# A Fourier mixing layer and hash-routed experts: another order of the head

## The chip, the cores and the metric

The kernel runs on one core of a Trainium2 chip. The metric is the device time of one execution in microseconds; the median of three runs is compared. The core has five engines that run their own instruction streams in order: TensorE (PE, with its weight loads as PEld), VectorE (DVE), ScalarE (ACT), GpSimd (POOL) and SyncE (SP). SP, ACT and POOL each also issue transfers into a queue of their own.

## The reference

```python
# x (8, 2496, 256); filt_r, filt_i (1249, 256)
X = np.fft.rfft(x, axis=1)
F = (filt_r + 1j * filt_i)[None, :, :]
y = np.fft.irfft(X * F, n=2496, axis=1).astype(np.float32)

x = y.reshape(19968, 256)                 # tokens
expert_idx = token_ids * np.int64(2654435761) % np.int64(8)
for e in range(8):                        # w1 (8, 256, 1024), w2 (8, 1024, 256)
    xe = x[expert_idx == e]
    out[expert_idx == e] = np.maximum(xe @ w1[e], 0.0) @ w2[e]
```

## The kernel before

**The mixing.** The transform of 2496 = 39 × 64 points is cut into three stages of matrix products, for each of 8 batches. *Stage 1* (`stage1`, product `pa`, line 185) multiplies by the 39-point table `wf_t`: eight units per batch, each of two products on one x piece of 312 KB, which ACT copies out (line 187) and stores into a DRAM buffer d1 (line 188, 320 KB). *Stage 2* (`stage2`) runs eleven steps: `forward` (product `pb`, line 202) multiplies groups loaded back from d1 (`load2`, line 194, two transfers of 256 KB per group of four frequencies) by `d_t`, VectorE multiplies by both filters (line 207), and `back` (product `pc`, line 221) multiplies by `e_t`; ACT copies (line 224) and stores into d2 (line 228). *Stage 3* (`stage3`, product `pd`, line 249) has eight units per batch: a piece of d2 (`load4`, line 239, 320 KB) is multiplied by `wi_t`, VectorE copies it out (line 251), and GpSimd scatters its four groups of 78 rows of 1088 bytes into `xs`, rows sorted by expert (`scatter`, line 257). A stage of a batch can start only when the stage before it has stored all of that batch, since its rows lie across. Rings of buffers: x 3, t1 2, t2 4, p 4, g 2, t4 3, o 2, PSUM for all three stages 4.

**The routing.** `route` computes on VectorE, from the token ids, where each token goes: expert ids, a mask that compares with `iota_e` (made on GpSimd, line 315), running counts, and two matmuls on PE for the counts over all partitions (lines 349 and 351, result `cnt_ps`, the second with the matrix `before` from GpSimd). A long chain on VectorE makes the slots of the tokens and stores them for the scatters (lines 397 and 398, GpSimd's queue); at its end `seg` goes through another matmul (line 436, `ce_ps`) into the experts of the 163 tiles, `chunk_i`. `dup_filters` then copies each filter table to the lower partitions, one on VectorE (line 447), one on ACT (line 448).

**The expert tiles.** 163 tiles of 128 tokens run in four stages; the tiles of the first stage (30) hold only tokens of batches 0 and 1, those of the second of batches up to 3, and so on. A tile loads its rows (`load`, line 515, four tiles ahead), turns them on PE (`turn`, line 523, `xps`), multiplies by w1 (`up`, line 534), ReLU on ACT and VectorE, by w2 (`down`, line 546), and scatters the result (line 550). `weights(i + 2, 0)` and `(i + 2, 1)` stand behind `up(i)` and `down(i)` on SP's queue and load 1 MB each if the expert changes; their buffers come free when `up(i)` and `down(i)` have run.

**The order.** It is written out by hand: each engine runs its instructions as the program emits them. `part1`, `part2` and `part3` give the units of a batch's stage a time, and their loads an earlier one; `pre` is the sorted list that is emitted ahead of the tiles, and `main` the one of which the pieces with a time below i + 1 stand in tile i, between `turn(i + 1)` and `down(i)`. `pre` holds batch 0's stage 1, `route`, batch 1's stage 1 mixed with batch 0's stage 2, then batch 1's stage 2 with batch 0's stage 3, then batch 1's stage 3 with batch 2's stage 1. Ahead of `pre`, SP loads `wf_t` and three x pieces, and ACT the token ids, a routing table, `d_t` (1.3 MB), four filter pieces (0.65 MB each), `e_t` (2.6 MB) and `wi_t`.

Of the kernel before, what the change touches and what calls it, by code (L numbers as in the profile page):

```python
# [20 lines left out]
B, S, C = 8, 2496, 256  # L21
# [11 lines left out]
NU = N2 // 2 // XG  # L33
# [75 lines left out]
def kernel(  # L109
# [159 lines left out]
    def weights(i, which):  # L269

        if i >= NT:
            return
        if i < 2:
            if which == 0:
                ws[i] = [wpool.tile([P, DP, F], F32, name=f"w1_{i}"), wpool.tile([P, FP, C], F32, name=f"w2_{i}")]
        elif which == 0:
            ws[i] = ws[i - 2]
        e = nc.sync.value_load(chunk_i[0:1, 0, i:i + 1], min_val=0, max_val=E - 1)
        kw = {}
        if i >= 2:  # L280
            kw = {"cond": nc.sync.value_load(chunk_i[0:1, 1, i:i + 1], min_val=0, max_val=1)}
        if which == 0:
            nc.sync.dma_start(out=ws[i][0][:], in_=moe_w1[bass.ds(e, 1)].rearrange("one (dp p) f -> p (one dp) f", p=P), **kw)
        else:
            nc.sync.dma_start(out=ws[i][1][:], in_=moe_w2[bass.ds(e, 1)].rearrange("one (fp p) d -> p (one fp) d", p=P), **kw)
# [13 lines left out]
    for k, filt in enumerate((filt_r, filt_i)):  # L299
        for q in range(2):  # L300
            off, step = (0, C) if q == 0 else (N1 * C, -C)
            nc.scalar.dma_start(
                out=f_t[k][32 * q:32 * q + 32, :, :],
                in_=bass.AP(tensor=filt.tensor, offset=filt.offset + off,
                            ap=[[N1 * C, 32], [step, NS], [1, C]]))
    nc.scalar.dma_start(out=e_t[:], in_=e_dram.ap())
    nc.scalar.dma_start(out=wi_t[:], in_=wi_dram.ap())

    make_identity(nc, ident[:])
    before = rpool.tile([P, P], F32)  # L310
# [12 lines left out]

        return ap.unsqueeze(2).to_broadcast([P, E, n])

    def route():

        eid_i = rpool.tile([P, NJ], I32)
        nc.vector.tensor_scalar(eid_i[:], tok[:, :, 0], E - 1, None, op0=OP.bitwise_and)
# [2 lines left out]
        mask = rpool.tile([P, E, NJ], F32)  # L332
# [3 lines left out]
        run = rpool.tile([P, E, NJ], F32)  # L336
# [3 lines left out]
        ends = rpool.tile([P, E + 1], F32)  # L340
# [7 lines left out]
        ps = fps.tile([P, 2, C], F32, name="cnt_ps", tag="f")  # L348
        nc.tensor.matmul(out=ps[:, 0, 0:G * E], lhsT=ones[:, 0:P], rhs=cntg[:].rearrange("p g e -> p (g e)"),
                         start=True, stop=True)  # L350
        nc.tensor.matmul(out=ps[:, 1, 0:E], lhsT=before[:], rhs=cnt[:], start=True, stop=True)

        upto = rpool.tile([P, G, E], F32)
# [20 lines left out]
        step = rpool.tile([P, G, E], F32)  # L376
# [33 lines left out]
        at = rpool.tile([P, NQP], F32)  # L410
# [17 lines left out]
        seg = rpool.tile([P, 2], F32)  # L428
# [2 lines left out]
        nc.vector.tensor_copy(seg_i[:], seg[:])  # L431
        nc.vector.tensor_scalar(seg_i[:], seg_i[:], E - 1, None, op0=OP.bitwise_and)
        nc.vector.tensor_copy(seg[:], seg_i[:])
        ps = fps.tile([P, 2, C], F32, name="ce_ps", tag="f")
        for q in range(2):
            nc.tensor.matmul(out=ps[0:1, 0, q * P:(q + 1) * P], lhsT=seg[:, q:q + 1], rhs=ident[:],
# [15 lines left out]
    def part1(b, t0, t1):  # L452
        bt = batches[b]
        at = [t0 + (t1 - t0) * u / NU for u in range(NU)]
        step = (t1 - t0) / NU
        out_ = [(at[u], lambda u=u: bt.stage1(u)) for u in range(NU)]
        out_ += [(at[u] - 1.9 * step, lambda u=u: bt.load1(u)) for u in range(3 if b == 0 else 0, NU)]
        return out_

    def part2(b, t0, t1, ready):  # L460
        bt = batches[b]
        n = NS // 2 + 1
        at = [t0 + (t1 - t0) * u / n for u in range(n)]
        step = (t1 - t0) / n
        out_ = [(at[u], lambda u=u: bt.stage2(u)) for u in range(n)]
        out_ += [(max(at[2 * g] - 4.5 * step, ready), lambda g=g: bt.load2(g)) for g in range(NS // SG)]
        return out_

    def part3(b, t0, t1):
        bt = batches[b]  # L470
        at = [t0 + (t1 - t0) * u / NU for u in range(NU)]
        step = (t1 - t0) / NU
        out_ = [(at[u], lambda u=u: bt.stage3(u)) for u in range(NU)]
        out_ += [(at[u] - 1.9 * step, lambda u=u: bt.load4(u)) for u in range(NU)]
        return out_

    order = stage_tiles()
    tiles = sum(order, [])
    stage_of = [g for g, o in enumerate(order) for _ in o]

    pre = part1(0, -100, -81) + [(-80.9, route), (-80.8, dup_filters)]
    pre += part1(1, -79, -60) + part2(0, -75, -50, -80)
    pre += part2(1, -45, -25, -59) + part3(0, -44, -25)
    pre += part3(1, -20, -1) + part1(2, -19, -2)
    pre += [(-30 + i, lambda i=i: (weights(i, 0), weights(i, 1))) for i in range(2)]
    pre.sort(key=lambda t: t[0])

    bounds = [0.0, 9.0, 18.0, 25.0, 44.0, 63.0, 84.0, 101.0]
    main, ready = [], 0.0
    for k, b in enumerate(range(3, B + 2)):  # L490
        t0, t1 = bounds[k], bounds[k + 1]
        d = t1 - t0
        if b - 1 < B:
            main += part2(b - 1, t0 + 0.01 * d, t0 + 0.9 * d, ready)
        if b < B:
            main += part1(b, t0 + 0.02 * d, t0 + 0.62 * d)
            ready = t0 + 0.65 * d
        if b - 2 >= 2:
            main += part3(b - 2, t0 + 0.3 * d, t1)
    main.sort(key=lambda t: t[0])  # L500

    for _, piece in pre:
# [98 lines left out]
```

## Time and profile before

| | us |
|---|---|
| median of three runs | 1775.54 (1774.68 to 1778.44) |
| the profiled execution | 1772.01 |
| its span, first to last instruction | 1770.3 |
| PE busy | 1665.8 (94%) |
| VectorE, ScalarE, GpSimd busy | 463.8, 222.9, 427.2 |

The span lies 1.7 us below the profiled execution's own time, and that execution 3.5 us below the median. Where a profile row says busy, a fraction of a stretch is meant in which at least one instruction of the engine runs; matmuls overlap at their ends, so the time from start to start is what one adds.

### The profile page before, as it was taken

The page shows a single profiled execution, that of the slowest core. Times are in us where ns is not written, and L with a number is a line of the kernel's source. Part 1 is how long each engine was busy: PE and PEld are TensorE (multiplying, and loading weights), DVE is VectorE, ACT ScalarE, POOL GpSimd, SP SyncE. Part 2 cuts the span into 40 slices and gives each one's busy share as a digit, 9 for nine tenths or more (in the row PEclk, how much of TensorE's full clock was granted, in tenths as well). Part 3 has the DMA queues.
Part 4 walks back from the last instruction along what each step waited for, and adds up shares of the span by engine and source line. Part 5 has one row for each costly group of instructions (what it writes and reads, how often), then busy time and mean ns, then how long its engine had stood idle before and what let it go on. Part 6 is the DMA issues. An engine that isn't in the chain of part 4 may idle for free.

```text
span 1770.3 us, 27290 instructions
## 1 busy us (share of the span) xinstructions
PE 1665.8 (94%) x9630; PEld 1390.9 (79%) x9630; DVE 463.8 (26%) x848; ACT 222.9 (13%) x373; POOL 427.2 (24%) x503
## 2 busy tenths in 40 slices
PE   3398778999999999999999999999999999999998
PEld 0165226887787888888888988898889999999997
DVE  1634212222323322222232222322222111121111
ACT  0231111212111111101110000100000000000000
POOL 0024540012424412230233123233431111111111
PEclk9998659999999999999999999999999999999999
DMA  9378846557667685446463564434516132322220
GB/s 218 101 205 210 261 125 152 160 162 225 184 195 217 175 264 182 128 121 194 123 196 98 160 197 125 123 108 125 187 52 228 62 111 68 104 78 89 83 81 12
DMA packets 159122, 260.72 MB, mean 147 GB/s; under 512 B 18351, under 2 KB 121536, under 8 KB 158667
## 3 DMA queue, kind: packets, MB, share of 16 engines
q1 hardware_dynamic: 108459, 166.93, 32.6%
q10 hardware_dynamic: 29984, 48.70, 9.9%
q0 software_dynamic: 20544, 43.36, 7.5%
q8 instruction: 77, 1.26, 0.3%
q14 instruction: 58, 0.48, 0.1%
HBM read 433.78 MB, written 86.09 MB: 294 GB/s over the span
## 4 chain that ended last, share of the span: by engine, by line
PE 70%; issue 20%; DMA 5%; POOL 3%; DVE 2%; POOLq 0%; ACT 0%; SPq 0%; ACTq 0%; DVEq 0%
PE ups L534 22%; PE dps L546 21%; PE pc L221 8%; PE pa L185 7%; PE pd L249 7%; PE pb L202 4%; POOL out_dram L550 3%; DMA d<-t 2%; PE xps L523 1%; DMA x<-in_x_dram 1%; DMA t<-d 1%; DMA d<-g 1%; DMA w<-in_moe_w_dram 0%; DVE acc L391 0%; DVE tmp L390 0%
## 5 line engine op out<-in xcount | busy, mean ns | idle before, releaser
L534 PEld LDWEIGHTS ups<-xt,w 128*128 128x128 f32 x5216 | 610.2, 192 | 9.3 <-DVE xt L525 0.9
L534 PE MATMUL ups<-xt,w 128*128 128x128 f32 x5216 | 611.0, 276 | 0.5 <-DVE xt L525 0.5
L546 PE MATMUL dps<-w,ht 128*128 128x256 f32 x2608 | 589.8, 379 | 0.0
L546 PEld LDWEIGHTS dps<-w,ht 128*128 128x128 f32 x2608 | 488.5, 190 | 80.3 <-issue 19.2
L550 POOL DMA_INDIRECT out_dram<-osb,xg x163 | 159.9, 981 | 904.7 <-DVE osb L549 878.2
L257 POOL DMA_INDIRECT xs<-o,sidx x256 | 240.9, 941 | 344.4 <-issue 197.6
L540 DVE TENSOR_SCALAR ht<-ups 128x512 f32<-128x512 f32 x163 | 112.8, 692 | 525.8 <-PE ups L534 522.2
L538 ACT ACTIVATE ht<-ups 128x512 f32<-128x512 f32 x163 | 97.3, 597 | 1021.7 <-PE ups L534 998.4
L549 DVE COPY osb<-dps 128x256 f32<-128x256 f32 x163 | 69.3, 425 | 506.7 <-PE dps L546 506.7
L185 PE MATMUL pa<-x,wf_t 78*80 78x512 f32 x256 | 152.2, 731 | 30.5 <-ACT t L187 22.7
L249 PE MATMUL pd<-t,wi_t 80*78 80x512 f32 x256 | 136.2, 658 | 18.8 <-DMA t<-d 18.8
L221 PE MATMUL pc<-p,e_t 128*128 128x256 f32 x640 | 152.2, 381 | 0.2 <-ACT g L224 0.2
L221 PEld LDWEIGHTS pc<-p,e_t 128*128 128x128 f32 x640 | 121.8, 191 | 18.1 <-ACT g L224 0.6
L185 PEld LDWEIGHTS pa<-x,wf_t 78*80 78x80 f32 x256 | 45.1, 181 | 105.2 <-issue 65.8
L207 DVE TENSOR_TENSOR p<-pb,filt 128x512 f32<-128x512 f32 x160 | 103.0, 686 | 87.1 <-PE pb L202 87.0
L251 DVE COPY o<-pd 78x512 f32<-78x512 f32 x128 | 87.6, 686 | 114.0 <-PE pd L249 69.6
L187 ACT COPY t<-pa 80x512 f32<-80x512 f32 x128 | 73.2, 581 | 224.4 <-PE pa L185 199.0
L249 PEld LDWEIGHTS pd<-t,wi_t 80*78 80x78 f32 x256 | 40.1, 163 | 74.1 <-issue 68.5
L202 PEld LDWEIGHTS pb<-t,d_t 128*128 128x128 f32 x320 | 60.8, 195 | 42.9 <-issue 30.8
L202 PE MATMUL pb<-t,d_t 128*128 128x256 f32 x320 | 85.0, 389 | 8.4 <-DMA t<-d 8.4
L224 ACT COPY g<-pc 128x512 f32<-128x512 f32 x80 | 46.8, 585 | 268.4 <-PE pc L221 235.7
L523 PE MATMUL xps<-ident,xg 128*128 128x128 f32 x326 | 62.5, 274 | 8.4 <-DMA xg<-xs 8.4
(76 smaller groups left out, 183.4 us busy)
## 6 DMA issues: line engine op xcount, KB each, us to landing
w<-in_moe_w_dram SPq DMA_DIRECT2D x326, 1024.0 KB
xg<-xs SPq DMA_DIRECT2D x163, 136.0 KB
d<-t ACTq DMA_DIRECT2D x64, 320.0 KB
t<-d SPq DMA_DIRECT2D x80, 256.0 KB
d<-g ACTq DMA_DIRECT2D x80, 256.0 KB
t<-d SPq DMA_DIRECT2D x64, 320.0 KB
x<-in_x_dram SPq DMA_DIRECT2D x64, 312.0 KB
xs<-o,sidx POOLq DMA_INDIRECT x256, 3.2
```

The costliest lines, as they stand in the source:

```text
L185: nc.tensor.matmul(out=ps[0:NK], lhsT=wf_t[:], rhs=xt[:, 2 * i:2 * i + 2, :], start=True, stop=True)
L202: nc.tensor.matmul(out=ps[:, i, :], lhsT=d_t[:, s, :], rhs=self.t2[s // SG][:, s % SG, :], start=True, stop=True)
L207: nc.vector.tensor_tensor(out=pt[:], in0=ps[:], in1=f_t[k][:, 2 * u:2 * u + 2, :], op=OP.mult)
L221: nc.tensor.matmul(out=ps[:, i, :], lhsT=e_t[:, k, 2 * u + i, :], rhs=pr[k][:, i, :], start=(k == 0), stop=(k == 1))
L249: nc.tensor.matmul(out=ps[0:NR], lhsT=wi_t[:], rhs=t4[:, 2 * i:2 * i + 2, :], start=True, stop=True)
L251: nc.vector.tensor_copy(out=o[:, 2 * i:2 * i + 2, 0:C], in_=ps[0:NR])
L257: st = nc.gpsimd.indirect_dma_start(out=xs[:], out_offset=bass.IndirectOffsetOnAxis(ap=index, axis=0), in_=rows, in_offset=None, bounds_ch ...
L534: nc.tensor.matmul(out=ps[:, k, :], lhsT=w1[:, dp, fp * P:(fp + 1) * P], rhs=xt[i][:, dp, :], start=(dp == 0), stop=(dp == DP - 1))
L538: nc.scalar.activation(out=dst, in_=ps[:], func=AF.Relu)
L540: nc.vector.tensor_scalar_max(dst, ps[:], 0.0)
L546: nc.tensor.matmul(out=ps[:], lhsT=ht[:, fp, :], rhs=w2[:, fp, :], start=(fp == 0), stop=(fp == FP - 1))
L550: st = nc.gpsimd.indirect_dma_start(out=out[:], out_offset=bass.IndirectOffsetOnAxis(ap=xg[i][:, C:C + 1].bitcast(I32), axis=0), in_=o[:], ...
```

## The change

The six transfers of the filters, `e_t` and `wi_t` are issued by GpSimd and no longer by ACT. `route` is cut in three: `count` (to the two count matmuls), `route` (the slots, to `seg`) and `experts` (from the `ce_ps` matmul on). `count` and `route` stand behind the first unit of batch 0's stage 1, `experts` late in batch 0's stage 2. In `pre`, stage 1 of batch 2, stage 2 of batch 1 and stage 3 of batch 0 are mixed, and stage 2 of batch 2 with stage 3 of batch 1. Batch 2's stage 3 is now the first of `main`, with batch 3's stage 1, and the times of the other stages among the tiles are written out anew.

```diff
@@ the loads ahead of pre
         for q in range(2):
             off, step = (0, C) if q == 0 else (N1 * C, -C)
-            nc.scalar.dma_start(
+            nc.gpsimd.dma_start(
                 out=f_t[k][32 * q:32 * q + 32, :, :],
...
-    nc.scalar.dma_start(out=e_t[:], in_=e_dram.ap())
-    nc.scalar.dma_start(out=wi_t[:], in_=wi_dram.ap())
+    nc.gpsimd.dma_start(out=e_t[:], in_=e_dram.ap())
+    nc.gpsimd.dma_start(out=wi_t[:], in_=wi_dram.ap())
...
-    def route():
+    rv = {}
+
+    def count():
...
+        rv.update(mask=mask, run=run, ends=ends, ps=ps)
+
+    def route():
+        mask, run, ends, ps = rv["mask"], rv["run"], rv["ends"], rv["ps"]
...
+        rv.update(seg=seg)
+
+    def experts():
+        seg = rv["seg"]
         ps = fps.tile([P, 2, C], F32, name="ce_ps", tag="f")
...
-    def part3(b, t0, t1):
+    def part3(b, t0, t1, ready):
...
-        out_ += [(at[u] - 1.9 * step, lambda u=u: bt.load4(u)) for u in range(NU)]
+        out_ += [(max(at[u] - 1.9 * step, ready), lambda u=u: bt.load4(u)) for u in range(NU)]
...
-    pre = part1(0, -100, -81) + [(-80.9, route), (-80.8, dup_filters)]
-    pre += part1(1, -79, -60) + part2(0, -75, -50, -80)
-    pre += part2(1, -45, -25, -59) + part3(0, -44, -25)
-    pre += part3(1, -20, -1) + part1(2, -19, -2)
+    pre = part1(0, -100, -81) + [(-99, count), (-98.9, route), (-60, experts), (-80.8, dup_filters)]
+    pre += part1(1, -79, -62) + part2(0, -77, -52, -80)
+    pre += part1(2, -50, -30) + part2(1, -50, -25, -61) + part3(0, -48, -27, -51.9)
+    pre += part2(2, -22, -1, -25) + part3(1, -20, -2, -24.9)
...
-    bounds = [0.0, 9.0, 18.0, 25.0, 44.0, 63.0, 84.0, 101.0]
...
+    main = part1(3, 0.1, 6) + part3(2, 0.2, 6, -0.9)
+    main += part2(3, 6.2, 13.5, 6.1) + part1(4, 6.5, 13)
+    main += part2(4, 14.2, 24, 13.2) + part1(5, 14.5, 22) + part3(3, 15, 25, 13.6)
...
```

On GpSimd, at the program's start; rows with a plus are those of the change, line numbers are its own:

```order
+L600 UNCONDITIONAL_BRANCH
+L302 DMA filt_105<-in_filt_r_dram 32x5120
+L302 DMA filt_105<-in_filt_r_dram 32x20x256
+L302 DMA filt_106<-in_filt_i_dram 32x5120
+L302 DMA filt_106<-in_filt_i_dram 32x20x256
+L306 DMA e_t<-e_tbl 128x5120
+L307 DMA wi_t<-wi_tbl 80x78
 masks.py:197 MEMSET ident 128x128
 masks.py:199 ISA
```

Six transfers stand ahead of the identity, and so ahead of `before` and `iota_e`, which follow it.

On PE, from the last unit of batch 0's stage 1 on, in the kernel before (pa and x are followed by the piece's number within its batch):

```order
L185 MATMUL pa_7_0_215<-x_7_202,wf_t 80x512
L185 MATMUL pa_7_1_218<-x_7_202,wf_t 80x512
L349 MATMUL cnt_ps<-cntg,ones 128x32
L351 MATMUL cnt_ps<-cnt,before 128x8
L436 MATMUL ce_ps<-ident,seg 1x128 x2
L185 MATMUL pa_0_0_364<-x_0_212,wf_t 80x512
L185 MATMUL pa_0_1_367<-x_0_212,wf_t 80x512
```

And in the change, from the program's start:

```order
L185 MATMUL pa_0_0_147<-x_0_114,wf_t 80x512
L185 MATMUL pa_0_1_150<-x_0_114,wf_t 80x512
L351 MATMUL cnt_ps<-cntg,ones 128x32
L353 MATMUL cnt_ps<-cnt,before 128x8
L185 MATMUL pa_1_0_275<-x_1_116,wf_t 80x512
L185 MATMUL pa_1_1_278<-x_1_116,wf_t 80x512
```

The count moved from behind the eighth unit to behind the first, and the `ce_ps` matmul, which waited right behind it, into batch 0's stage 2.

On PE, behind the last product of batch 1's stage 2 in the kernel before (the first number of pd, pa, t4 and x is the batch, the second the piece):

```order
L249 MATMUL pd_1_0_0_985<-t4_1_0_975,wi_t_102 78x512
L249 MATMUL pd_1_0_1_988<-t4_1_0_975,wi_t_102 78x512
L185 MATMUL pa_2_0_0_1007<-x_2_0_977,wf_t_101 80x512
L185 MATMUL pa_2_0_1_1010<-x_2_0_977,wf_t_101 80x512
L249 MATMUL pd_1_1_0_1018<-t4_1_1_979,wi_t_102 78x512
L249 MATMUL pd_1_1_1_1021<-t4_1_1_979,wi_t_102 78x512
```

And where batch 2's stage 1 stands in the change, behind batch 0's stage 2:

```order
L185 MATMUL pa_2_1_0_667<-x_2_1_602,wf_t_101 80x512
L185 MATMUL pa_2_1_1_670<-x_2_1_602,wf_t_101 80x512
L202 MATMUL pb_1_2_679<-t2_1_1_589,d_t_103 128x256 x2
L221 MATMUL pc_1_1_686<-p_1_1_0_654,e_t_104 128x256
L221 MATMUL pc_1_1_686<-p_1_1_1_656,e_t_104 128x256
L221 MATMUL pc_1_1_686<-p_1_1_0_654,e_t_104 128x256
L221 MATMUL pc_1_1_686<-p_1_1_1_656,e_t_104 128x256
L249 MATMUL pd_0_1_0_696<-t4_0_1_609,wi_t_102 78x512
L249 MATMUL pd_0_1_1_699<-t4_0_1_609,wi_t_102 78x512
```

Before, units of stages 3 and 1 alternate alone; now each stands among those of stage 2.

## Rows read from the trace of the kernel before

**Rows 1.** The page: PE's busy time, its 40 slices, the granted clock.
```profile
PE 1665.8 (94%) x9630; PEld 1390.9 (79%) x9630; DVE 463.8 (26%) x848; ACT 222.9 (13%) x373; POOL 427.2 (24%) x503
...
PE   3398778999999999999999999999999999999998
...
PEclk9998659999999999999999999999999999999999
```

**Rows 2.** Stretches: length, busy time by engine, granted clock, DMA share, GB/s.
```profile
0.00:57.90 57.90, 27.41 (x32) 7.58 (x33) 5.41 (x9) 9.56 (x16) 1.53 (x11) 1.00 0.86 207
57.90:90.20 32.30, 2.62 (x10) 1.43 (x9) 27.88 (x56) 5.04 (x2) 2.72 (x3) 1.00 0.27 67
90.20:136.10 45.90, 45.63 (x157) 29.72 (x156) 16.86 (x26) 14.76 (x26) 8.71 (x7) 1.00 0.77 216
...
143.55:186.30 42.75, 42.73 (x148) 28.28 (x148) 20.76 (x32) 5.26 (x9) 26.41 (x33) 0.92 0.90 254
186.30:197.55 11.25, 0.00 (x0) 0.03 (x1) 1.28 (x2) 0.58 (x1) 5.33 (x8) 0.74 0.84 264
197.55:252.45 54.90, 54.87 (x64) 16.25 (x64) 10.30 (x15) 9.30 (x16) 27.93 (x36) 0.50 0.62 173
252.45:260.86 8.41, 0.00 (x0) 0.03 (x1) 0.69 (x1) 0.00 (x0) 3.62 (x4) 0.50 0.26 77
260.86:289.00 28.14, 19.21 (x77) 14.61 (x78) 4.03 (x7) 3.51 (x6) 0.00 (x0) 0.77 0.60 139
289.00:1762.30 1473.30, 1473.30 (x9147) 1292.93 (x9145) 374.87 (x697) 174.92 (x297) 349.98 (x402) 1.00 0.47 141
```

**Rows 3.** The timeline of PE among the tiles: start, length, instruction.
```profile
304.34 1.88 PE L185 MATMUL pa<-x,wf_t 78*80 78x512 f32 x4
306.06 1.03 PE L202 MATMUL pb<-t,d_t 128*128 128x256 f32 x4
306.92 1.89 PE L221 MATMUL pc<-p,e_t 128*128 128x256 f32 x8
308.65 1.88 PE L185 MATMUL pa<-x,wf_t 78*80 78x512 f32 x4
...
413.51 1.88 PE L249 MATMUL pd<-t,wi_t 80*78 80x512 f32 x4
```

**Rows 4.** The timeline of ACT in batch 0's stage 1 (brackets: idle before, releaser).
```profile
19.63 0.32 ACTq L307 DMA_DIRECT2D wi_t<-wi_tbl  x1
...
21.28 1.06 ACT L187 COPY t<-pa 80x512 f32<-80x512 f32 x2
...
44.34 1.06 ACT L187 COPY t<-pa 80x512 f32<-80x512 f32 x2 [20.55 <-DMA d<-t]
```

**Rows 5.** The timeline of POOL, VectorE and PE at the routing and the scatters.
```profile
86.25 0.90 POOL L398 DMA_DIRECT2D sidx<-slots  x1 [2.29 <-DMA slots<-slot_i]
...
89.26 1.01 PE L436 MATMUL ce_ps<-ident,seg 128*1 128x128 f32 x4 [29.68 <-DVE seg L433]
...
91.51 2.82 DVE L447 COPY filt<-filt 64x5120 f32<-64x5120 f32 x1
91.57 3.60 POOL L257 DMA_INDIRECT xs<-blank,at_i  x1 [0.30 <-issue]
...
192.20 0.94 POOL L257 DMA_INDIRECT xs<-o,sidx  x1 [0.30 <-issue]
```

**Rows 6.** The timeline of PE and of SP's queue where stages meet.
```profile
97.11 1.91 PE L202 MATMUL pb<-t,d_t 128*128 128x256 f32 x4
...
131.59 3.62 PE L221 MATMUL pc<-p,e_t 128*128 128x256 f32 x16
...
139.94 0.80 SPq L239 DMA_DIRECT2D t<-d  x2
...
143.55 3.67 PE L249 MATMUL pd<-t,wi_t 80*78 80x512 f32 x4 [7.49 <-DMA t<-d]
...
276.75 2.05 PE L202 MATMUL pb<-t,d_t 128*128 128x256 f32 x4 [8.41 <-DMA t<-d]
```

More of the change, by code (lines that the diff above doesn't have):

```diff
@@ L479 @@
     stage_of = [g for g, o in enumerate(order) for _ in o]
-    pre = part1(0, -100, -81) + [(-80.9, route), (-80.8, dup_filters)]
-    pre += part1(1, -79, -60) + part2(0, -75, -50, -80)
-    pre += part2(1, -45, -25, -59) + part3(0, -44, -25)
-    pre += part3(1, -20, -1) + part1(2, -19, -2)
+    pre = part1(0, -100, -81) + [(-99, count), (-98.9, route), (-60, experts), (-80.8, dup_filters)]
+    pre += part1(1, -79, -62) + part2(0, -77, -52, -80)
+    pre += part1(2, -50, -30) + part2(1, -50, -25, -61) + part3(0, -48, -27, -51.9)
+    pre += part2(2, -22, -1, -25) + part3(1, -20, -2, -24.9)
     pre += [(-30 + i, lambda i=i: (weights(i, 0), weights(i, 1))) for i in range(2)]
     pre.sort(key=lambda t: t[0])
-    bounds = [0.0, 9.0, 18.0, 25.0, 44.0, 63.0, 84.0, 101.0]
[L489 to L499, printed above, removed]
+    main = part1(3, 0.1, 6) + part3(2, 0.2, 6, -0.9)
+    main += part2(3, 6.2, 13.5, 6.1) + part1(4, 6.5, 13)
+    main += part2(4, 14.2, 24, 13.2) + part1(5, 14.5, 22) + part3(3, 15, 25, 13.6)
+    for b, t0 in ((5, 25.2), (6, 44.2)):
+        main += part2(b, t0, t0 + 17, t0 - 2) + part1(b + 1, t0 + 0.4, t0 + 12) + part3(b - 1, t0 + 5, t0 + 18.5, t0)
+    main += part2(7, 63.2, 80, 61) + part3(6, 67, 83, 62) + part3(7, 84, 101, 81)
     main.sort(key=lambda t: t[0])
```

## The prediction

> **What bounds the kernel now.** I read the page first: TensorE (PE) is busy 94% of the span and its slices are full from the eighth on; only the first seven are not, and the granted clock is below 1.0 in some of these [rows 1]. So I cut the span at the head's own turning points and took the busy time of each stretch [rows 2]. From 289 us to the last matmul PE is busy 1473.30 of 1473.30 us at clock 1.00. Nothing that the change does there can help; all that can be won is what PE loses before 289.
>
> To price that loss I need the work at the 2.4 GHz level. Among the tiles, from start to start, a stage-1 unit (pa) takes 306.06 − 304.34 = 1.72 us, pb 0.86, pc 308.65 − 306.92 = 1.73 [rows 3]; a stage-3 unit (pd) is as busy as a pa (1.88), so 1.72 too. A batch therefore holds 8 × 1.72 = 13.8 us of stage 1, 10 × 2.59 = 25.9 of stage 2, 13.8 of stage 3: 53.5 in all. Stretch less work gives the **ledger of before** [rows 2]: batch 0's stage 1, 57.9 − 13.8 = 44.1; waiting for the routing, 32.3; stage 1 of batch 1 with stage 2 of batch 0, 45.9 − 40.6 = 5.3; idle 7.5 [rows 6]; stage 2 of batch 1 with stage 3 of batch 0, 42.75 − 38.8 = 3.9; idle 11.25; stage 3 of batch 1 with stage 1 of batch 2, 54.9 − 27.6 = 27.3; idle 8.4; tile 0, with a stretch of 8.41 in which PE waits for stage 2's load [rows 6], 28.1 − 14.3 = 13.8. Sum: **153.8 us lost**. The change is priced by a second ledger with the same units.
>
> **The change, part by part.**
>
> *Stage 1 of batch 0 (A).* In before, ACT hands out six table transfers until 19.95 and copies only from 21.28; its first two stores stand behind the tables in its own queue, and the next copy waits 20.55 us for them [rows 4]. After the change these six stand on POOL, ACT keeps three, and its stores stand behind d_t alone. POOL pays: a plain transfer cost it 0.90 us [rows 5], so six with 0.3 us between them some 7 us, ahead of the identity, `before` and iota_e. The routing's mask needs iota_e, so the count's matmul, now second on PE, comes at about 1 + 7 + 1 + 5.4 (VectorE's nine instructions of the first stretch [rows 2]) = 15; pa_1 to pa_7, queued behind it, start there and no longer right behind pa_0. What binds next is bytes: tokens 0.16 MB, d_t 1.31, filters 2.62, e_t 2.62, x 2.56, stores 2.62, two x units of batch 1 0.64: 12.5 MB. Before moved 207 GB/s in this stretch [rows 2]: 60.5 us with e_t ahead of the stores, 47.9 if e_t comes last. I take 54, plus 4 for the load of stage 2's first group (139.94 to 143.55 in before [rows 6]): pb_0 of batch 0 at **58**. Bounds: 46, where PE's half-speed pace decides (15 + 7 × 3.44 + 3.6 for the load and as much for the last store), and 66. Work done by then is 13.8 + 1.7, so **42.5 lost** (30 to 50).
>
> *The routing.* PE waited 29.68 us for VectorE's chain to end in `seg` [rows 5]. Now this chain runs from about 16 to 46, beside A's transfers; nothing waits for it but the filters' copy and the first products, due at 59. Its cost is 0 while A lasts to 49; the full 29.7 if the count came late (a rival below). So the 32.3 us fall out.
>
> One GpSimd scatter took 3.60 us and not 0.94 beside VectorE's 2.82 us copy of the filters [rows 5]. The Trainium skill (SBUF — State Buffer, section "SBUF: two separate sides") says that such a copy locks GpSimd out of writing descriptors, and advises the ACT or SP queue instead, which speaks against this change; by it as by the row the loss would be 2.7 us on POOL wherever the two meet, and in the first 8 us VectorE has only the two short steps on the token ids to run, so the sum would not move.
>
> *Batch 1's stage 1 with batch 0's stage 2 (B).* The same mixture took 97.11 to 135.2 in before [rows 6] and holds one more unit now. I add 3 for a start at 1.2 GHz: 43 us for 38 of work, **5 lost** (2 to 8). It ends at 101.
>
> *To batch 0's stage 3.* From the last pc's end to the first pd, through store and load, took 143.55 − 135.2 = 8.3 us [rows 6]. Now pa and pb (2.6) fill part: 5.7 idle, and 3 at the lower clock, which the same place shows: **8.7** (6 to 10).
>
> *Three stages mixed (C).* 53.5 us of PE work, 15.8 MB for a batch's three stages, and of the weights' 4.2 MB about half. That is 17.9 MB in some 62 us, 288 GB/s, where the best stretches moved 254 at a share of 0.90 and 264 at 0.84 [rows 2], that is 282 to 314 at a full share. So C is near the limit of the transfers: **6 lost**, between 0 and 22 (all the weights at 254 GB/s).
>
> *To batch 2's stage 2.* SP's queue holds the weights, then batch 2's first groups, then batch 1's load for stage 3. Before paid 11.25 here with the weights just as late; one load group more stands ahead and 3.4 us of work fills: 9 idle and 3 of low clock, **12** (6 to 18).
>
> *Stage 2 of batch 2 with stage 3 of batch 1 (D).* Before lost 3.9 with the same mixture, clock included: **2** (0 to 6). The stretch of stages 1 and 3 alone is gone: there PE was busy 54.87 of 54.9 us at clock 0.50 [rows 2] and lost 27.3.
>
> *To tile 0.* Before needed 8.4 from the end of PE's work; with scatters trailing as at 192.20, 6 us behind the mixture's end [rows 5, 6], it would be 10.5. One pc now stands behind the last pd: **9** (6 to 12).
>
> *Among the tiles.* Batch 2's stage 3 and batch 3's stage 1 now meet in tile 0. SP issues their first loads only once up(0) has freed the weights' buffer. I count 3.4 for up(0) at the lower clock as before, 4.5 for x, and since pa and pd, alternating alone, ran at 1.2 GHz throughout [rows 2], 6.9 for these four and 2.5 for the start of the down product. In tile 6 batch 3's stage 2 is loaded in the tile that uses it, as batch 2's was in tile 0, where 8.41 us were lost [rows 6]: 8 with the clock. Together **25.3** (12 to 32), where before has 13.8.
>
> **Sum:** 42.5 + 5 + 8.7 + 6 + 12 + 2 + 9 + 25.3 = 110.5 against 153.8, a gain of 43.3 us. The profiled execution took 1772.0 (span 1770.3): 1728.7. The median lies 3.5 above that execution, so the forecast is **1732** (1712 to 1752 by the middle of the bounds).
>
> **Rivals.**
>
> *The transfers bind.* The stores of A end with the last table byte wherever tables are issued, C pays for all weights, and the load behind it too: A +8, C +16, the gap +6, 30 us of the 43 given back: **1762**. For it speaks the share of 0.86 in A and 0.90 later [rows 2]; against it, that the copy's 20.55 us were order within one queue, not bytes. The Trainium skill (DMA: Bandwidth & Descriptors, section "Issuing engines are not separate DMA queues") says that all issuers share the same 16 engines and that another issuer saves only issue time; by that rule A would end at the 66 above, and the trace so far shows both, ACT held until 19.95 and bytes at a share of 0.86.
>
> *The gaps fill.* A by its low end (30), no loss in C, 7 behind it, 14 among the tiles: 12.5 + 6 + 5 + 11.3 = 35 more, **1697**. For it: ample work of a third batch at every wait.
>
> *Slower: the lower clock through the mixture.* Where pa and pd stood alone the clock stayed at 1.2 GHz though PE was never idle. In C they are 27.6 of 53.5 us, in B and D a third. If short waits for transfers and this share keep 1.2 GHz through C and D, their remaining 90.6 us double; less the 6 already counted, 85 more: **1817**. It turns the gain into a loss from the point where over half of that work (43 us) runs at 1.2 GHz. Against it, the mixture from 143.55 shows 0.92 over 42.75 us [rows 2]: 6.8 us at 0.50, the rest at 1.00.
>
> *Nothing won: POOL is held as ACT was.* ACT needed until 19.95 for these transfers [rows 4]. If POOL must wait for room until the tables have landed, near 55, iota_e, the count and seven units of stage 1 come behind that and A ends near 100: about **1774**.
>
> **How the numbers follow.** Forecast 0.54, gaps fill 0.18, transfers bind 0.17, nothing won 0.05, slower 0.06. Two in ten may be left out: the lower clock, nothing won and the outer halves of the first two rivals go, and the range is 1702 to 1760. About 0.2% (3.5 us) is what a measurement of this kernel can tell from no change. Faster 0.89 (the first three), same 0.05, slower 0.06.
>
> **What would show it.** Right: ACT's first copy before 12 us; the count's matmul near 15; no wait of PE for `seg`; pb_0 near 58; the first tile's transposes near 232 with three batches' stage 2 done; clock 1.00 through most of C. Wrong: POOL's iota_e after 20 us (nothing won); PE waits on loads spread all through C with a DMA share over 0.9 (transfers bind); clock 0.50 in C or D (slower); waits of PE in tiles 0 and 6 that differ from 4.5 and 6 move the last term. If PE should be idle again behind 300 us, my assumption that the rest of the kernel stays as it is would be wrong.

## The result, and the profile after

The change runs in 1732.01 us (median of four, 1729.24 to 1736.04) against 1775.52 (1774.68 to 1778.44): a ratio of 0.9754, 95% interval 0.9729 to 0.9779, 43.5 us. The forecast was 1732. The two profiled executions differ by less: spans of 1734.3 and 1770.3 us, 36.0 apart. The profiled execution of the kernel before lies 3.5 below its median, that of the change (1736.04) is the slowest of its four. So the ledger, which was made against one execution, promised 43.3 and is to be held against 36.0. The 3.5 us below the one median and the 4.0 above the other make 43.5 of the 36.0; that the median is met to the tenth is luck.

The page of the change, PE's busy time, its 40 slices and the granted clock (before: [rows 1]):

```profile
PE 1658.3 (96%) x9630; PEld 1390.2 (80%) x9630; DVE 462.6 (27%) x848; ACT 223.0 (13%) x373; POOL 428.3 (25%) x509
...
PE   5889869899999999999999999999999999999998
...
PEclk9999969899999999999999999999999999999999
```

The head now cut at its new turning points (before: [rows 2]). Columns: stretch, length, busy time of PE, PEld, VectorE, ACT, POOL with their instructions, granted clock, DMA share, GB/s:

```profile
0.00:59.80 59.80, 33.59 (x40) 8.99 (x41) 35.98 (x66) 15.81 (x20) 13.95 (x27) 1.00 0.89 242
59.80:105.25 45.45, 45.43 (x152) 29.95 (x152) 13.92 (x25) 13.21 (x23) 0.00 (x0) 1.00 0.80 208
105.25:115.47 10.22, 2.94 (x10) 1.31 (x9) 1.29 (x2) 1.75 (x3) 0.00 (x0) 0.93 0.86 227
115.47:170.50 55.03, 54.26 (x176) 31.77 (x176) 22.28 (x34) 13.30 (x23) 29.57 (x37) 0.95 1.00 298
170.50:176.93 6.43, 0.16 (x1) 0.03 (x1) 0.00 (x0) 0.58 (x1) 2.08 (x3) 0.90 1.06 264
176.93:224.20 47.27, 43.78 (x152) 28.78 (x152) 23.04 (x36) 5.27 (x9) 26.90 (x34) 0.94 0.72 187
224.20:234.03 9.83, 0.13 (x2) 0.04 (x1) 0.00 (x0) 0.58 (x1) 4.83 (x7) 0.63 0.52 137
234.03:265.72 31.69, 26.36 (x68) 15.29 (x69) 4.20 (x7) 2.92 (x5) 7.72 (x9) 0.58 0.53 134
...
347.00:1726.30 1379.30, 1378.70 (x8669) 1220.41 (x8668) 342.39 (x644) 157.25 (x267) 312.44 (x356) 1.00 0.45 136
```

Up to 105 us the clock column reads 1.00 whatever the products do: four matmuls of stage 1 take 3.67 us in batch 0 and 1.88 from 73.47 on. There their lengths tell the level, and "half speed" is said by them.

With the prediction's units (pa, pd 1.72 us, pb 0.86, pc 1.73) the third ledger reads:

| us lost | before | predicted | measured in the change |
|---|---|---|---|
| batch 0's stage 1, to pb_0 (A) | 44.1 | 42.5 | 59.8 − 15.5 = 44.3 |
| waiting for the routing | 32.3 | 0 | 0 |
| batch 1's stage 1 with batch 0's stage 2 (B) | 5.3 | 5 | 45.45 − 38.0 = 7.5 |
| to batch 0's stage 3 | 7.5 | 8.7 | 10.2 − 2.6 = 7.6 |
| three stages mixed (C) | 3.9 | 6 | 55.0 − 50.9 = 4.1 |
| to batch 2's stage 2, and D | 11.25 + 27.3 | 12 + 2 | 6.43 + 47.27 − 39.7 = 14.0 |
| to tile 0 | 8.4 | 9 | 9.8 |
| tile 0 (and tile 6 in the change) | 13.8 | 17.3 + 8 | 17.3 + 12.5 |
| sum | 153.8 | 110.5 | 117.1 |

Before's mixtures are other ones, as the prediction tells. The difference of the sums, 36.7, is that of the spans (36.0) within a microsecond. Behind 347 us PE is busy 1378.70 of 1379.30 us. All of this is the first measurement of the change; a later one, on another chip, stands below.

The start, in the timeline of all engines (start, length, engine, instruction; in brackets the idle time before and what ended it; before: [rows 4, 5]):

```profile
1.38 1.48 POOL L302 DMA_DIRECT2D filt<-in_filt_r_dram  x2 [0.86 <-POOLq L591]
...
6.19 0.14 POOL L315 IOTA iota_e<- 128x8 f32 x1
...
7.89 0.58 ACT L187 COPY t<-pa 80x512 f32<-80x512 f32 x1 [4.34 <-PE pa L185]
...
11.31 0.64 PE L351 MATMUL cnt_ps<-cntg,ones 128*128 128x32 f32 x2 [1.75 <-DVE cntg L348]
```

GpSimd hands out the six tables between 1.38 and 5.10 us and is not held; ACT's first copy comes at 7.89 instead of 21.28 [rows 4]; the count's matmul stands at 11.31. ACT still waits for its stores later in A (5.60, 6.55 and 5.27 us, `d<-t`), but nowhere for 20.55.

The waits of PE that are left, from its timeline (before: [rows 5, 6]):

```profile
40.29 14.32 PE L185 MATMUL pa<-x,wf_t 78*80 78x512 f32 x16 [4.12 <-DMA x<-in_x_dram]
59.82 2.04 PE L202 MATMUL pb<-t,d_t 128*128 128x256 f32 x4 [5.21 <-DMA t<-d]
...
73.47 1.88 PE L185 MATMUL pa<-x,wf_t 78*80 78x512 f32 x4
...
97.71 0.60 PE L446 MATMUL ce_ps<-ident,seg 128*1 128x128 f32 x4
...
115.47 3.67 PE L249 MATMUL pd<-t,wi_t 80*78 80x512 f32 x4 [5.24 <-DMA t<-d]
...
176.93 3.75 PE L202 MATMUL pb<-t,d_t 128*128 128x256 f32 x8 [6.27 <-DMA t<-d]
180.48 2.85 PE L221 MATMUL pc<-p,e_t 128*128 128x256 f32 x8
...
198.64 1.94 PE L249 MATMUL pd<-t,wi_t 80*78 80x512 f32 x4 [1.57 <-DVE o L251]
...
213.21 1.13 PE L202 MATMUL pb<-t,d_t 128*128 128x256 f32 x4 [1.24 <-DVE o L251]
...
234.03 0.66 PE L527 MATMUL xps<-ident,xg 128*128 128x128 f32 x2 [9.70 <-DMA xg<-xs]
235.20 6.32 PE L538 MATMUL ups<-xt,w 128*128 128x128 f32 x32 [0.52 <-DVE xt L529]
...
246.55 3.67 PE L185 MATMUL pa<-x,wf_t 78*80 78x512 f32 x4 [4.81 <-DMA x<-in_x_dram]
...
260.25 5.63 PE L550 MATMUL dps<-w,ht 128*128 128x256 f32 x16
...
334.81 2.05 PE L202 MATMUL pb<-t,d_t 128*128 128x256 f32 x4 [8.29 <-DMA t<-d]
...
347.48 3.73 PE L538 MATMUL ups<-xt,w 128*128 128x128 f32 x32
```

The wait for `seg` (29.68 us before) is gone: `ce_ps` runs at 97.71 without one. In its place stand shorter waits: four where a stage, or the tiles, begin with rows that have only just been stored (59.82, 115.47, 176.93, 234.03), one for a load that SP issues only behind a transfer of weights whose buffer `up(6)` frees (334.81), and one for x in tile 0, with products at half speed behind each of them; the two for VectorE's copy-out are small.

### The profile page after: what moved, and what is told of

It is laid out like the page before. It is cut to its first block, busy times and chain, and to the rows that moved or that the text cites. A ratio compares the mean times of both kernels' runs of the same rounds, so it can differ in the third digit from the quotient of the medians.

```text
span 1734.3 us, 27336 instructions
## 1 busy us (share of the span) xinstructions
PE 1658.3 (96%) x9630; PEld 1390.2 (80%) x9630; DVE 462.6 (27%) x848; ACT 223.0 (13%) x373; POOL 428.3 (25%) x509
## 4 chain that ended last, share of the span: by engine, by line
PE 64%; issue 24%; DMA 7%; POOL 4%; DVE 0%; POOLq 0%; SPq 0%; ACT 0%; ACTq 0%; DVEq 0%
PE ups L538 20%; PE dps L550 20%; PE pc L221 7%; PE pa L185 6%; PE pd L249 6%; PE pb L202 4%; POOL out_dram L554 4%; DMA x<-in_x_dram 2%; PE xps L527 1%; DMA w<-in_moe_w_dram 1%; DMA xs<-o,sidx 1%; DMA t<-d 1%; POOL xs L257 1%; DMA d<-g 1%; DVE o L251 0%
## 5 line engine op out<-in xcount | busy, mean ns | idle before, releaser
L185 PE MATMUL pa<-x,wf_t 78*80 78x512 f32 x256 | 144.8, 697 | 26.1 <-DMA x<-in_x_dram 26.0
L207 DVE TENSOR_TENSOR p<-pb,filt 128x512 f32<-128x512 f32 x160 | 102.9, 685 | 113.5 <-PE pb L202 113.3
L249 PE MATMUL pd<-t,wi_t 80*78 80x512 f32 x256 | 125.8, 614 | 7.4 <-DMA t<-d 5.2
L185 PEld LDWEIGHTS pa<-x,wf_t 78*80 78x80 f32 x256 | 41.9, 171 | 91.9 <-issue 75.3
L202 PE MATMUL pb<-t,d_t 128*128 128x256 f32 x320 | 89.0, 404 | 21.0 <-DMA t<-d 19.8
```

The costliest lines, as they stand in the source:

```text
L185: nc.tensor.matmul(out=ps[0:NK], lhsT=wf_t[:], rhs=xt[:, 2 * i:2 * i + 2, :], start=True, stop=True)
L202: nc.tensor.matmul(out=ps[:, i, :], lhsT=d_t[:, s, :], rhs=self.t2[s // SG][:, s % SG, :], start=True, stop=True)
L207: nc.vector.tensor_tensor(out=pt[:], in0=ps[:], in1=f_t[k][:, 2 * u:2 * u + 2, :], op=OP.mult)
L249: nc.tensor.matmul(out=ps[0:NR], lhsT=wi_t[:], rhs=t4[:, 2 * i:2 * i + 2, :], start=True, stop=True)
```

## Experiments

They ran on three chips, each set with the kernel before beside it: the first four kernels where it takes 1774.09 us, the next four where it takes 1793.91 (the second chip below), the last four where it takes 1787.38 (the third). Whole times of different sets are compared by their ratio alone.

### The parts of the change, one at a time

**Tables alone.** The kernel before, with nothing but the tables' issuer changed:

```diff
-            nc.scalar.dma_start(          # filters, four times
+            nc.gpsimd.dma_start(
-    nc.scalar.dma_start(out=e_t[:], in_=e_dram.ap())
-    nc.scalar.dma_start(out=wi_t[:], in_=wi_dram.ap())
+    nc.gpsimd.dma_start(out=e_t[:], in_=e_dram.ap())
+    nc.gpsimd.dma_start(out=wi_t[:], in_=wi_dram.ap())
```

> Before with only the six table transfers on GpSimd's queue. Theory (queue order and bytes): stage 1 of batch 0 ends near 51 and not at 58.7, since its stores no longer stand behind the tables, but PE then waits some 30 us for VectorE's routing chain as before: 7 us gained, about 1768. Rival (the tables' queue is the main part of the gain): stage 1 ends by 40 and 18 us or more are gained, 1757 or less.

Measured: 1766.58 us, ratio 0.996 (0.9946 to 0.9974), 7.5 us less, as the theory had it. ACT's timeline, then PE's:

```profile
40.86 1.06 ACT L187 COPY t<-pa 80x512 f32<-80x512 f32 x2 [6.22 <-DMA d<-t]
```

```profile
41.34 10.50 PE L185 MATMUL pa<-x,wf_t 78*80 78x512 f32 x12 [4.42 <-DMA x<-in_x_dram]
...
82.20 1.01 PE L436 MATMUL ce_ps<-ident,seg 128*1 128x128 f32 x4 [29.71 <-DVE seg L433]
```

With the same bytes on another queue, ACT's longest wait for a store falls from 20.55 us [rows 4] to 6.22. Stage 1 of batch 0 ends at 51.8 instead of 58.9, the routing stays where it is behind it (29.71 us again), and `ce_ps` comes 7.1 us earlier. That is nearly the whole gain; the rest of ACT's wait was covered.

**Tables and early routing**, the order of the stages as before (`part3`'s floor is put out of the way):

```diff
-    pre = part1(0, -100, -81) + [(-80.9, route), (-80.8, dup_filters)]
+    pre = part1(0, -100, -81) + [(-99, count), (-98.9, route), (-60, experts), (-80.8, dup_filters)]
...
-    pre += part2(1, -45, -25, -59) + part3(0, -44, -25)
-    pre += part3(1, -20, -1) + part1(2, -19, -2)
+    pre += part2(1, -45, -25, -59) + part3(0, -44, -25, -200)
+    pre += part3(1, -20, -1, -200) + part1(2, -19, -2)
```

> Before with the tables on GpSimd's queue and count and routing behind the first unit, the order of the stages otherwise as before. Theory (the gain is in batch 0's stage 1 and the routing, the mixing gives back what it wins): the first pb near 60 and 36 us gained, about 1740. Rival (the mixing carries a good part, above all the 27.3 us that stages 1 and 3 lose at the lower clock): at most 20 us gained, 1755 or more.

Measured: 1747.64 us, 0.9852 (0.9835 to 0.9868), 26.5 us less: theory (36) and rival (at most 20) both fall; it lies between.

**Early routing alone**, the same edit with the tables on ACT:

> Before with only count and routing behind the first unit, tables on ACT. Theory: PE's wait of 29.68 us for seg goes; batch 0's stage 1 still ends at 58.7 and its loads land near 67, so 28 us gained, about 1748. Rival (the routing chain on VectorE only moves the wait, since the filters' copy and the products queue behind it): under 12 us gained, 1764 or more.

Measured: 1750.96 us, 0.9878 (0.9861 to 0.9896), 23.1 us less: the rival falls, and the theory's 28 are not reached. PE's timeline of this kernel, then of the one with the tables on GpSimd too:

```profile
46.04 20.77 PE L185 MATMUL pa<-x,wf_t 78*80 78x512 f32 x24 [17.89 <-ACT t L187]
68.56 2.04 PE L202 MATMUL pb<-t,d_t 128*128 128x256 f32 x4 [1.75 <-DMA t<-d]
72.46 3.67 PE L185 MATMUL pa<-x,wf_t 78*80 78x512 f32 x4 [1.85 <-DMA x<-in_x_dram]
...
120.66 3.67 PE L249 MATMUL pd<-t,wi_t 80*78 80x512 f32 x4 [7.59 <-DMA t<-d]
```

```profile
41.81 17.32 PE L185 MATMUL pa<-x,wf_t 78*80 78x512 f32 x20 [4.26 <-DMA x<-in_x_dram]
61.79 2.04 PE L202 MATMUL pb<-t,d_t 128*128 128x256 f32 x4 [2.66 <-DMA t<-d]
```

With the tables on ACT, PE does wait 17.89 us for the stores behind them, and without that it waits 4.26 for x; yet stage 2 starts only 6.8 us earlier in the second kernel, and the time falls by 3.3, which the intervals do not tell from nothing. While PE stood, x pieces went on loading, and the units behind the wait run without a gap. Of the 6.8 us, 6.4 are still there at batch 2's first pb in tile 0 (247.06 against 253.47) and 3.2 at the `up` behind it (262.39 against 265.62): with the tables on ACT the clock came back in the first pa there, with the tables on GpSimd not before the first pc.

**The mixture alone**: the times of `pre` and `main` of the change, with tables on ACT and the routing in one piece behind batch 0's stage 1:

```diff
+    pre = part1(0, -100, -81) + [(-80.92, count), (-80.91, route), (-80.9, experts), (-80.8, dup_filters)]
```

> The change's mixing of the stages alone: tables on ACT, count, routing and experts behind batch 0's stage 1 as before. Theory (by the two ledgers the mixing is worth 1 to 3 us): 1770 to 1776. Rival (the mixing saves the 27.3 us of the lower clock): 1750 or less.

Measured: 1759.43 us, 0.9916 (0.9899 to 0.9933), 14.7 us less. Theory and rival both fall; it lies between. The routing's wait is there as before (29.71 us). PE's timeline:

```profile
259.11 0.66 PE L527 MATMUL xps<-ident,xg 128*128 128x128 f32 x2 [10.05 <-DMA xg<-xs]
...
271.93 3.67 PE L185 MATMUL pa<-x,wf_t 78*80 78x512 f32 x4 [4.73 <-DMA x<-in_x_dram]
```

The tiles start 1.8 us earlier than in the kernel before (260.86 [rows 2]) and with batch 2's stage 2, 25.9 us of work, done already: 27.7 won in the head. In tiles 0 and 6 the waits of the change are back (4.73, and 8.22 at 360.36), and there it loses 17.9 and 12.6 us, where the kernel before loses 13.8. 27.7 − 16.7 = 11.0. The spans of the two profiled executions, 1770.3 and 1759.3, lie just that apart; the medians give 14.7.

So of the change's 43.5 us the early routing gives some 23, the tables 3 more beside it (not clear of the noise), the mixture 15. 26.5 + 14.7 = 41.2: within the intervals the parts add up. So they do by the spans of the profiled executions: 25.8 for tables and routing (1744.5) and 11.0 for the mixture, against 36.0.

### What is lost in tiles 0 and 6

**Tile 6.** Batch 3's stage 2 is loaded one tile earlier:

```diff
-    main += part2(3, 6.2, 13.5, 6.1) + part1(4, 6.5, 13)
+    main += part2(3, 6.2, 13.5, 5.3) + part1(4, 6.5, 13)
```

> The change with batch 3's stage 2 loads issued one tile earlier (tile 5, not tile 6). Theory (SP frees the loads only behind up(6), so PE waits 8.29 us and then runs about 4 us of work at 1.2 GHz): 12 us less than the change, about 1720. Rival (the transfers are late whenever they are issued, the DMA share being high): under 4 us less, 1728 or more.

**Tile 0.** The first units of `main` one tile later:

```diff
-    main = part1(3, 0.1, 6) + part3(2, 0.2, 6, -0.9)
+    main = part1(3, 1.1, 6) + part3(2, 1.2, 6, 0.0)
```

> The change with the first units of batch 3's stage 1 and batch 2's stage 3 one tile later, their loads in tile 0. Theory (4.81 us of waiting for x, and pa and pd alone keep 1.2 GHz for 6.9 us more): 10 to 12 us less than the change, about 1721, the clock back at 1.0 within tile 0's down product. Rival (the clock stays low for as long after the gap whatever runs): only the wait goes, 5 us less, about 1727.

**Both**, with 5.5 as the time of the load:

> Both of these shifts. Theory: they add, 22 to 24 us less than the change, about 1709. Rival (a wait taken away in one tile comes back in the next, since the loads of both share SP's queue): 12 us less or fewer, 1720 or more.

| | time | ratio to before | tile 0's transposes to batch 3's first pb | and to the `up` behind it |
|---|---|---|---|---|
| the change, first measurement | 1732.01 | 0.9754 | 334.81 − 234.03 = 100.8 | 347.48 − 234.03 = 113.5 |
| tile 6 | 1741.09 | 0.9699 (0.9666 to 0.9733) | 335.15 − 242.09 = 93.1 | 343.85 − 242.09 = 101.8 |
| tile 0 | 1748.14 | 0.9750 (0.9724 to 0.9775) | 328.66 − 237.24 = 91.4 | 342.30 − 237.24 = 105.1 |
| both | 1733.20 | 0.9664 (0.9628 to 0.9701) | 320.87 − 237.69 = 83.2 | 329.57 − 237.69 = 91.9 |

Each of the two stretches holds the same work every time; on the third chip the change takes 101.7 and 114.1 us for them. Up to the first pb it is 7.7 us less by the one edit, 9.4 by the other, 17.6 by both. The second stretch also holds the products at half speed behind that pb: 11.7, 8.4 and 21.6 less, where 12, 10 to 12 and 22 to 24 were expected. That pair of losses is what it was read to be, and the rivals fall.

The whole time follows for tile 6 and for both, by the ratios 9.9 and 16.1 us against 0.9754, which another chip gave; for tile 0 alone the ratio does not move (its interval would allow 5 us), and that run settles only the stretch, not the total. Part of what is missing stands in the traces: behind 375 us PE waits 8.3 us in the tile 6 run, 8.7 in the tile 0 run and 12.3 with both, nearly always ahead of `down` for ACT's ReLU and at most 1.4 us at a time. The first measurement of the change has no such wait there. What makes them was not tried. PE's timeline with tile 6 mended, with tile 0 mended, and with both:

```profile
335.15 1.10 PE L202 MATMUL pb<-t,d_t 128*128 128x256 f32 x4 [0.46 <-issue]
...
343.85 3.73 PE L538 MATMUL ups<-xt,w 128*128 128x128 f32 x32
```

```profile
251.76 1.88 PE L185 MATMUL pa<-x,wf_t 78*80 78x512 f32 x4
...
256.91 1.88 PE L249 MATMUL pd<-t,wi_t 80*78 80x512 f32 x4
...
328.66 2.05 PE L202 MATMUL pb<-t,d_t 128*128 128x256 f32 x4 [9.68 <-DMA t<-d]
```

```profile
329.57 3.73 PE L538 MATMUL ups<-xt,w 128*128 128x128 f32 x32
```

The same four units of stages 1 and 3 take 13.7 us in the change's tile 0 and 6.9 in tile 1 of the second run (251.76 on). They are not slow by themselves: in the change they follow an idle 4.81 us at the lower clock and don't raise it, in the second run they follow tile 0's products at 2.4 GHz and keep it.

**A third batch's stage 1 into the last stretch.** Batch 3's stage 1 moves ahead of the tiles, among batch 2's stage 2 and batch 1's stage 3:

```diff
-    pre += part2(2, -22, -1, -25) + part3(1, -20, -2, -24.9)
+    pre += part2(2, -22, -1, -25) + part3(1, -20, -2, -24.9) + part1(3, -19, -0.5)
...
-    main = part1(3, 0.1, 6) + part3(2, 0.2, 6, -0.9)
-    main += part2(3, 6.2, 13.5, 6.1) + part1(4, 6.5, 13)
+    main = part3(2, 1.1, 8, 0.0)
+    main += part2(3, 1.2, 12, 0.0) + part1(4, 4, 12)
```

> The change with batch 3's stage 1 mixed into the last stretch ahead of the tiles (stage 2 of batch 2, stage 3 of batch 1), batch 3's stage 2 with batch 2's stage 3 from tile 1 on. Theory (that stretch lasts as long as GpSimd's 32 scatters, PE waits for them for 9.7 us and 3 more): the tiles start at most 5 us later, and 9 to 14 us more than with both shifts are gained, about 1698. Rival (PE or the transfers bind there): the tiles start 14 us later and the time is that of both shifts, 1708 or more.

Measured: 1724.19 us, 0.9601 (0.9582 to 0.962), 9.0 us less than with both shifts, the low end of the theory. The tiles start 10.0 us later than there (247.72 against 237.69), between the theory's 5 and the rival's 14. The change itself had not run on that chip, so it was put beside this kernel on another:

> The change itself, on the chip of the three runs beside it. If chips differ only by a factor, the ratio to the kernel before is the 0.9754 of the first measurement (0.973 to 0.978), and the three refinements of the last stretch and of tiles 0 and 6 stand against it on one chip. Rival: the second chip loses more where transfers are dense, so that the change is worth less on it: a ratio of 0.978 to 0.985, and the mixed stretch (three stages, 55 us with the transfer engines all but full in the first measurement) lasts 58 us or more.

Measured: 1748.41 us, 0.9773 (0.9751 to 0.9794), which agrees with 0.9754 within the intervals; the mixed stretch lasts 55.1 us (115.10 to 170.24), as in the first measurement (55.0), so the rival's loss in the mixture isn't seen. The tiles start 5.8 us later here (239.81 against 234.03), lost behind batch 2's first pb: PE waits 2.66 us for stage 3's load at 181.66 and 3.82 at 209.74, put down to ACT's copy, with products at half speed behind both, where the first measurement has no wait above 1.6 up to the scatters. Why this chip loses them there was not tried.

> Stage 1 of batch 3 in the last stretch ahead of the tiles, as run before at a ratio of 0.960 on a chip where the kernel before took 1793.9. Theory: what the change loses in tiles 0 and 6 (some 17 and 12.5 us) is all but gone, and the tiles start later by less than the 13.8 us of work moved ahead of them, so 24 to 28 us less than the change on the same chip, a ratio of 0.960 to 0.962. Rival (the gain on the other chip was that chip's): under 15 us less than the change, 0.967 or more.

Measured: 1714.90 us, 0.9589 (0.9574 to 0.9605), 33.5 us less than the change on the same chip, more than the 24 to 28 of the theory. Tile 0's transposes start 8.1 us later (247.88 against 239.81) with 13.8 us more work done ahead of them. So 5.7 us are won ahead of the tiles: this trace has no such stop as the change's at 209.74 on this chip. The other 27.8 are most of what the change loses in tiles 0 and 6 (30.2 here).

**The cover for the scatters.** On top of that, batch 1's stage 3 ends earlier, and the two other stages reach to the end:

```diff
-    pre += part2(2, -22, -1, -25) + part3(1, -20, -2, -24.9) + part1(3, -19, -0.5)
+    pre += part2(2, -22, -0.5, -25) + part3(1, -20.5, -6, -24.9) + part1(3, -18, -0.2)
```

> As the one before it, with batch 1's stage 3 ended earlier (four times in six of the stretch) and stages 2 and 1 of batches 2 and 3 stretched to its end. Theory: tile 0's transposes wait for the scatters of batch 1's last pieces, which trail the last product of stage 3 by some 9 us; with some 10 us of other products behind that, the wait of 8.4 us for the gathered rows falls to 1 to 4, and the time by 4 to 7 us, ratio 0.956 to 0.958. Rival: the products behind are stage 1's, which run at the lower clock and wait for x pieces at the end of SP's queue, so that what is won at the transposes is lost there: within 2 us of the one before it.

Measured: 1709.81 us, 0.9563 (0.9547 to 0.9580): 5.1 us less than the one before it, as the theory had it, 38.6 less than the change on this chip, and the best kernel here. PE's timeline of the two, the earlier one first:

```profile
247.88 0.66 PE L527 MATMUL xps<-ident,xg 128*128 128x128 f32 x2 [8.52 <-DMA xg<-xs]
```

```profile
227.25 1.88 PE L249 MATMUL pd<-t,wi_t 80*78 80x512 f32 x4
...
239.32 1.88 PE L185 MATMUL pa<-x,wf_t 78*80 78x512 f32 x4
241.39 0.41 PE L527 MATMUL xps<-ident,xg 128*128 128x128 f32 x2 [0.19 <-DMA xg<-xs]
242.31 3.84 PE L538 MATMUL ups<-xt,w 128*128 128x128 f32 x32 [0.52 <-DVE xt L529]
```

The last pd ends at 229.0, 12.4 us of other work stand behind it, and the gathered rows are there: 8.52 us of wait become 0.19, and `up` of the first tile runs in 3.84 us and not in 5.17, with next to no idle time ahead of it.

### Do bytes set the end of batch 0's stage 1?

```diff
-    e_t = cpool.tile([P, 2, NS, P], F32)
+    e_t = cpool.tile([P, 1, NS, P], F32)
...
-    nc.gpsimd.dma_start(out=e_t[:], in_=e_dram.ap())
+    nc.gpsimd.dma_start(out=e_t[:], in_=e_dram.ap()[:, 0:1])
```

> The change with only the first half of e_t loaded and used for both products of stage 2's last step (the filtered spectrum's second part is multiplied by the wrong table): 1.31 MB less ahead of stage 2, the same instructions on PE. Theory (bytes set the end of batch 0's stage 1): at the 242 GB/s of that stretch the first product of stage 2 starts 1.31 MB / 242 GB/s = 5.4 us earlier than in the change (59.8 there), and the time falls by about 5 us, ratio to the kernel before 0.0028 below that of the change. Rival (the ring of x pieces and PE at the lower clock set the pace, not bytes): the first product starts within 1 us of the change's, and the time is the same within 2 us.

Measured: 1741.75 us, 0.9746 (0.9728 to 0.9764), against 0.9773 for the change. PE's timeline with half of `e_t`, then that of the change on the same chip:

```profile
10.50 3.67 PE L185 MATMUL pa<-x,wf_t 78*80 78x512 f32 x4 [10.50 <-DMA x<-in_x_dram]
...
39.17 13.91 PE L185 MATMUL pa<-x,wf_t 78*80 78x512 f32 x16 [1.61 <-DMA x<-in_x_dram]
58.88 2.05 PE L202 MATMUL pb<-t,d_t 128*128 128x256 f32 x4 [5.79 <-DMA t<-d]
```

```profile
5.46 3.67 PE L185 MATMUL pa<-x,wf_t 78*80 78x512 f32 x4 [5.46 <-DMA x<-in_x_dram]
...
40.94 13.96 PE L185 MATMUL pa<-x,wf_t 78*80 78x512 f32 x16 [4.49 <-ACT t L187]
60.71 2.04 PE L202 MATMUL pb<-t,d_t 128*128 128x256 f32 x4 [5.81 <-DMA t<-d]
```

Stage 2 starts 1.8 us earlier, a third of the 5.4, so theory and rival both fall. The first x piece also came 5.0 us later in this run, which may hide a part; against that, in the tile 6 run above it came as late (10.15) and pb_0 stands at 61.99, where three others on that chip have 60.74 to 62.04. The ratio falls by 0.0027, as the theory had it, but the intervals overlap, and tile 0's transposes stand at 240.18 against 239.81, so the time settles nothing. What both traces show alike is the last third of A: four units at half speed (13.9 us) on end without a wait, and then 5.8 for store and load. In those 20 us the transfers are at a share of 0.74 and 0.76; there it isn't bytes that hold PE. In the first 40 us the share is 0.93 and 0.95, and PE waits mostly for x; how much of that is bytes stays open.

## Why the prediction was right, step by step

**Held.** PE's loss ahead of 289 us was all there was to win, and behind 347 nothing was lost or gained in the first measurement. The routing's wait went (29.68 of the 32.3 us; for 2.62 of them PE was busy [rows 2]), and POOL was not held ("nothing won" falls at iota_e, 6.19 us). The clock stayed up where stage 2 is in the mixture: 0.95 in C, 0.94 in D ("slower" falls). C was at a DMA share of 1.00 and 298 GB/s and PE still lost only 4.1 us: the transfers were as near their limit as the estimate of 288 said, and it did not cost what "transfers bind" asked for it (22). "Gaps fill" falls at A and the tiles. Tile 0's transposes came at 234.0 (forecast 232) and tile 0 lost the 17.3 forecast, by the steps forecast: the wait for x 4.81, four units at half speed.

**Right in the sum, wrong in the step.** pb_0 came at 59.8 for 58, but the count stood at 11.3, not 15: six transfers cost POOL 3.8 us and not 7, as they took 0.57 to 0.74 each where the row used had 0.90, with no 0.3 between them. pa_1 did start near 15, at 15.90, but because its x piece came only then (3.56 us of wait). SP issued the load of stage 2's first group when the last store had landed, in its timeline

```profile
54.81 2.66 SPq L194 DMA_DIRECT2D t<-d  x4
```

near the 54 of the forecast, and pb_0 came 5.0 us behind it, not 4. That 54 is luck in part: the bytes that were to set it don't act in the last 20 us, as above, where four units at half speed do.

The Trainium skill (DMA: Bandwidth & Descriptors, section "Issuing engines are not separate DMA queues") has it that another issuer saves issue time alone. In time gained, 7.5 us for the tables alone and 3.3 beside early routing, this case is near that rule. In the trace it is not issue time alone: ACT's longest wait for a store fell from 20.55 us to 6.22 with the same bytes on another queue. The waits that ended were mostly covered, so their length was no price.

**Terms that were mis-sized.** B lost 7.5 and not 5: the timeline has half speed from pb_0 at 59.8 on (its 2.04 us would be 1.03) and full speed only from 73.5. "To batch 0's stage 3" and C are split otherwise than forecast: the 7.6 is idle time alone (forecast 5.7), the slow start behind it (forecast 3) stands in C with 2.7, and of C's 4.1 that leaves 1.4, not 6; there "gaps fill" was nearly right. Tile 6 lost 12.5 and not 8, the largest miss: the wait was 8.29 where 6 were forecast, and the lower clock behind it cost 4.2 and not 2. "To batch 2's stage 2" and D lost 14.0 together as forecast, but split otherwise: the idle time is 6.4 and not 9, the slow start of stage 2 costs 3 as forecast (3.75 + 2.85 for 3.45 of work), and in D 4.5 are lost and not 2, 2.8 of it waiting for VectorE's copy-out (1.57 and 1.24).

**The attribution failed.** The ledger gives the routing 32.3 and all that the mixture does 9.5 (4.7 with the measured column); the single edits give 23 and 15. In the run with early routing alone, 28.6 us are there at batch 0's first pb (68.56 against 97.11 [rows 6]) and 22.9 at its first pd (120.66 against 143.55 [rows 6]). PE waits 1.75 us for the load ahead of that pb and 1.85 for x behind it, both of which the routing's wait had covered, and a unit of stage 1, a pb and part of a pc run at half speed behind that. In the change such losses came to light in A and B and were booked there. A ledger by stretches adds up, but an edit is not worth the stretch that it empties.

## What to carry to other kernels

When a long wait is taken away, price what it had covered: the next store-to-load path and the slow first microseconds behind it. At every point where a stage begins with rows that were just stored, put 5 to 10 us of another batch's work between the last store and the first use; mixing two stages only moves the gap, and here a third batch's work in the last stretch ahead of the tiles, with the scatters ended early, took another 38.6 us, in which what tiles 0 and 6 had lost is contained. Move loads one step earlier than the unit that uses them if they stand behind freed buffers in the same queue.

## What the runs showed of the hardware that was not expected

- The same products of stages 1 and 3 (78 × 80) run at either clock according to what came before: 3.4 us a unit for 54.9 us on end behind 11.25 us without work in the kernel before, at a granted 0.50 with PE busy 54.87 us [rows 2]; 1.72 us a unit behind products at 2.4 GHz. Where the clock rose in the change's head and first tiles, it rose in pb, pc, `up` or `dps` (180.48: 2.85 us for a pc that takes 3.45 or 1.73; 260.25: 5.63 for a `dps` that takes 3.62); with early routing alone it rose once in a pa, right behind a pb (255.31, 2.70 us). The Trainium skill (TensorE: Matmul & The Clock Gate, section "Part 1: The HAM clock gate (the "warmup" mystery)") lets the clock follow how busy PE has been. The trace of the kernel before does not show it so: in that stretch PE was busy throughout and the clock stayed down. Which property of these products decides was not tried.
- The store of the slots, now on a queue that has handed out 5.3 MB of tables and in a stretch with a DMA share of 0.89, took 7.53 us until the next transfer could start, where it took 2.29 before [rows 5]. PE did not wait for it; whether the queue or the load made it longer was not tried.
- Three chips ran the kernel before in 1774, 1787 and 1794 us. Ratios carried over better than times: 0.9754 and 0.9773 for the change, 0.9601 and 0.9589 for the kernel with a third batch's stage 1 ahead of the tiles. Small waits did not: those for ACT's ReLU behind 375 us come to 7.5 to 12.9 us in the four runs on the chip with 1794, to 1.7 for the change on the one with 1787, and to none in its first measurement.
